# First units of an HGRN2 and maxout-FFN kernel: two tokens a partition in the loads, x from outputs by tokens, and half FFN steps placed among units 2 and 3

## The chip, the cores and the metric

The kernel runs on one core of a Trainium2 chip. The metric is the device time of one execution in microseconds (us). The kernel before took 477.63 us (median of 3 runs, 477.24 to 480.0). All times below are from those runs or from one profiled execution.

## What is computed

A gated linear recurrence for 4 batches and 8 heads over 768 tokens with heads of 48 features; its outputs, gathered to `x` of 3072 tokens by 384, go through a feed-forward network (FFN) that takes the maximum of three products.

```python
f = 1.0 / (1.0 + np.exp(-f_logit))
for t in range(S):
    state = f[:, :, t, :, None] * state + np.einsum('bhd,bhe->bhde', k[:, :, t], v[:, :, t])
    y[:, :, t] = np.einsum('bhd,bhde->bhe', q[:, :, t], state)
x = np.ascontiguousarray(y.transpose(0, 2, 1, 3)).reshape(B * S, H * D)
h = np.maximum(np.maximum(x @ w1, x @ w2), x @ w3)
return h @ w_out
```

The weights are 384 by 768 (three of them) and 768 by 384, and arrive as 64-bit floats.

## The kernel before

**Units and groups.** The tokens are cut into 24 units. Unit u is chunk u // 2 of 64 tokens of the two batches 2(u % 2) and 2(u % 2) + 1, all heads. Four units make a group of 512 tokens. Each group has its own `xT` (features on partitions, tokens along the free axis) and its own FFN, which runs while the units of the next group are computed.

**One unit.** `load` brings f, k and q, `load_v` brings v. For units 0 to 7 (`u < BY_ROWS`) a load has tokens on partitions, `transposed` (L274) turns each of f, k and q by four TensorE transposes of 128x128 (L278) into PSUM, and later units are turned by VectorE instead. `sigmoids` (L295) makes the gate; `scan` and `before` run the two scans of VectorE (L316, L334); `after` makes kh (L327), `keys` transposes it on TensorE (L354) and copies it to ks. `pairs` multiplies kh and qh (L379) and masks the result to `at` (L382). `values` multiplies v with `at` (L393) and ks with v (L402) into one PSUM tile y, and adds the new state (L408, L410). `finish` adds the part of the old state (L423) and ScalarE copies y, feature by token, into `heads` in three pieces (L429).

**Packing.** In `heads` the features of a head lie on partitions 0 to 47 or 64 to 111. `pack` (L437) moves them to the dense feature order of `xT` by ten DMA transfers (L445). For group 0 units 0 and 1 are packed by one call and units 2 and 3 by another, all on the SP queue. In every later group `pack(0, 2)` comes after the third unit's `finish` and `pack(3, 3, xT, both)` after the fourth's, alternately on the queues of SP and ScalarE, five each.

**The FFN as a generator.** `ffn(g, xT)` (L453) issues its work in steps: for each of six column blocks j and three weights i three matmuls (L472) of 128x512, with a ScalarE copy (L477) or a VectorE maximum (L479) after them; then four output blocks of six matmuls (L497), each with a copy (L500) and two output DMAs (L505). A full step counts as two yields, an output block as two, so a group from the second on has 18 x 2 + 4 x 2 = 44. Group 0 does the blocks j = 0 and 1 in 12 half steps of 256 tokens, one yield each, first those of units 0 and 1, then those of units 2 and 3, so it has 12 + 12 x 2 + 8 = 44 yields as well. In group 0 each step also rounds weights (`round_begin` on ScalarE, L232; `round_end` on VectorE, L239 and L240, and GpSimd, L246) and issues the loads of more of them (`load_weights`, L208, 12 buffers).

**The order.** `tc.manual_schedule()` keeps the order of the code on each engine; nothing is reordered. `pending` holds the FFN generators in order and `fill(n)` takes n yields from the first; when it ends, the next begins. Units 0 to 3 are written out by hand (L535 to L602). There `busy(n)` puts in matmuls whose result is not used. Before the loop come `fill(6)`, `fill(2)`, `fill(2)`. The loop over u from 4 takes in each of the units 4 to 7 seven yields (2, 2, 2 and 1); in unit 8 eight, of which none is ahead of its `keys`; then 12 in odd and 10 in even units. The head of one turn of the loop sets where the next group's FFN may begin:

```python
fill(0 if u == 2 * GRP else 4 if u % 2 and u > 2 * GRP else 2)
...
    finish(u - 1)
    ...
    elif u % GRP == 0:
        pack(3, 3, xT, both)
if u % GRP == 0:
    if u > GRP:
        pending.append(ffn(u // GRP - 1, xT))
...
pairs(u)
...
fill(2)
```

After the loop come `fill(2)`, `finish(23)`, the last `pack(3, 3, xT, both)`, the last FFN appended, and `fill(12)`.

**Queues.** Nearly all DMAs are issued by SP in the order of the code; an SP instruction that waits holds all that follow. DMAs of SP and ScalarE take eight landing semaphores in turn, and an issue waits until the transfer that last had its semaphore has landed. Nine of the first weight loads go by GpSimd's queue (L571, L589, L594).

Of the kernel before, what the change touches and what calls it, by code (L numbers as in the profile page):

```python
# [9 lines left out]
FP32 = mybir.dt.float32  # L10
# [36 lines left out]
C = 64  # L47
DP = 64
# [7 lines left out]
def kernel(  # L56
# [32 lines left out]
    def fast():  # L89
        ctx = ExitStack()  # L90
        with ctx:
# [47 lines left out]
            ROOM = H * DP  # L139
            NAMES = "fkq"  # L140
            room = {nm: [keep.tile([128, 2 * ROOM], FP32, name=f"{nm}_ld{i}") for i in range(2)] for nm in NAMES}
            slots = {nm: [room[nm][u // 2][:, u % 2 * ROOM:(u % 2 + 1) * ROOM] for u in range(4)] for nm in NAMES}
            rows = {nm: [t.rearrange("t (h d) -> t h d", d=DP) for t in slots[nm]] for nm in NAMES}
            blocks = {nm: [t.rearrange("p (n h d) -> p n h d", n=C // 32, d=32) for t in room[nm]] for nm in NAMES}
            for nm in NAMES:
                for t in room[nm]:
                    nc.vector.memset(t.rearrange("p (h d) -> p h d", d=DP)[:, :, D:], 0.0)
# [10 lines left out]
            act = (nc.scalar, nc.scalar)  # L158

            def load_tokens(dst, src, u, queues=one):  # L160
                c, bp = divmod(u, 2)
                for a in range(2):
                    queues[a].dma_start(out=dst[a * C:(a + 1) * C, :, 0:D],  # L163
                                        in_=src[2 * bp + a, :, c * C:(c + 1) * C, :].rearrange("h t d -> t h d"))

            def load(u, queues=one, names="fkq"):
                for nm, src in (("f", f_logit), ("k", k), ("q", q)):
                    if nm not in names:
                        continue
                    if u < BY_ROWS:  # L170

                        c, bp = divmod(u, 2)
                        queues[NAMES.index(nm) % 2].dma_start(  # L173
                            out=rows[nm][u % 4][:, :, 0:D],
                            in_=src[2 * bp:2 * bp + 2, :, c * C:(c + 1) * C, :].rearrange("b h t d -> t b h d"))
                    elif u % 2 == 0:
                        t0 = u // 2 * C
                        for n in range(C // 32):
                            for par in range(2):
                                for e0, w in ((0, 32), (32, D - 32)):  # L180
                                    p0 = par * DP + e0
                                    nc.sync.dma_start(  # L182
                                        out=blocks[nm][u // 2 % 2][p0:p0 + 32, n, :, 0:w],
                                        in_=src[:, par::2, t0 + n * 32:t0 + (n + 1) * 32, e0:e0 + w].rearrange(
                                            "b h t d -> t (b h) d"))

            def load_v(u, queues=one):
                load_tokens(v_tiles[u % NLD], v, u, queues)
# [85 lines left out]
            def transposed(nm, u, name="tr"):  # L274

                t = {"tr": ps_tr, "p": ps_f}[name].tile([128, HP, 2, C], FP32, name=name)
                for hp in range(HP):
                    nc.tensor.transpose(t[:, hp].rearrange("p a t -> p t a"), slots[nm][u % 4][:, hp * 128:(hp + 1) * 128],  # L278
                                        ident)
                return t.rearrange("p h a t -> p a h t")  # L280
# [105 lines left out]
            def values(u):  # L386
# [3 lines left out]
                for hp in range(HP):  # L390
                    for par, a in FOUR:
                        o, s = (par ^ a) * DP, slice(a * C, (a + 1) * C)
                        nc.tensor.matmul(y[o:o + DP, a, hp * C:(hp + 1) * C], lhsT=v_ld[s, 2 * hp + par, :],  # L393
                                         rhs=d["at"][s, par, hp, :], start=(hp == 0),
                                         stop=False, skip_group_check=True)
                if u < NU - 2:

                    Y = HP * C
                    for hp in range(HP):
                        for par, a in FOUR:  # L400
                            s = slice(a * C, (a + 1) * C)
                            nc.tensor.matmul(y[par * DP:(par + 1) * DP, a, Y + hp * D:Y + (hp + 1) * D],  # L402
                                             lhsT=d["ks"][s, 2 * hp + par, :], rhs=v_ld[s, 2 * hp + par, 0:D],
                                             start=False, stop=(hp == HP - 1), skip_group_check=True)
# [6 lines left out]
                d["y"] = y  # L411

            heads = keep.tile([128, HP, TOK], FP32, name="heads")

# [22 lines left out]
            def pack(u0, u1, xT, queues=one, half=None):  # L437

                t, n = slice(u0 * UT, (u1 + 1) * UT), 0
                to = xT[:, :, t] if half is None else by_halves(xT)[:, half]  # L440
                for h in range(H):
                    for lo, hi in ((h * D, min(h * D // 128 * 128 + 128, h * D + D)), (h * D // 128 * 128 + 128, h * D + D)):
                        if lo < hi:
                            p0 = h % 2 * DP + lo - h * D
                            queues[n % len(queues)].dma_start(out=to[lo % 128:lo % 128 + hi - lo, lo // 128, :],  # L445
                                                    in_=heads[p0:p0 + hi - lo, h // 2, t])
                            n += 1
# [86 lines left out]
            with tc.manual_schedule():  # L534
                load(0, both)  # L535
                load(1, (nc.scalar, nc.sync))
                load_v(0)
                load(2, one, "f")
                load_v(1)
                load(2, one, "kq")  # L540
                load(3)
                load_v(2)
                load_v(3)
                xT = new_xT()
# [13 lines left out]
                keys(1)  # L558
                scan(2)
                after(2)  # L560
                pairs(1)
                finish(0)
                carry(2)
                before(2)
                sigmoids(3)
                busy(2)
                values(1)
                keys(2)
                scan(3)
                after(3)  # L570
                load_weights(6, queue=nc.gpsimd)  # L571
                pairs(2)
                finish(1)
                carry(3)
                pack(0, 1, xT, one, 0)
                load(GRP, one, "fk")
                before(3)
                busy(2)
                values(2)
                keys(3)  # L580
                round_begin(0)
                finish(2)
                pairs(3)
                round_end(0)
                busy(2)
                round_begin(1)
                round_begin(2)
                round_end(1)
                load_weights(2, queue=nc.gpsimd)  # L589
                values(3)  # L590

                nc.tensor.transpose(ps_tr.tile([128, 128], FP32, name="tr"), ident, ident)
                round_end(2)
                load_weights(1, queue=nc.gpsimd)  # L594
                finish(3)
                round_begin(3)
                pack(2, 3, xT, one, 1)
                load_weights(3)
                load(GRP, one, "q")
# [3 lines left out]
                pending.append(ffn(0, xT))  # L603
# [8 lines left out]
                for u in range(GRP, NU):  # L612
# [18 lines left out]
                    if BY_ROWS <= u + 3 < NU and u % 2:  # L631
                        load(u + 3, one, "fkq" if u % GRP == 1 else "f")
# [13 lines left out]
                    if BY_ROWS <= u + 2 < NU and u % GRP == 0:  # L646
                        load(u + 2, one, "k")
# [9 lines left out]
                    if BY_ROWS <= u + 2 < NU and u % GRP == 0:  # L657
                        load(u + 2, one, "q")
# [270 lines left out]
```

## Time and profile before

| what | value |
|---|---|
| median of 3 runs | 477.63 us (477.24 to 480.0) |
| profiled execution: its time, its span | 478.4 us, 476.7 us |
| TensorE busy (PE) | 456.6 us, 96% of the span |
| VectorE, ScalarE, GpSimd busy | 270.4 us, 146.0 us, 109.9 us |
| FFN matmuls L472, L497 | 293.1 us, 96.3 us |
| transfers xT<-heads, all | 120 |
| HBM read, written | 37.75 MB, 4.72 MB |

PE is TensorE's matmul side, PEld its weight loads, DVE VectorE, ACT ScalarE, POOL GpSimd, SP the engine that issues most DMAs; a "q" behind the name means the engine's instruction queue (waits and DMA issues). Views that the prediction uses: the slices (the span in 40 parts, digits are tenths busy), the windows (busy us of each engine in a stretch, with the granted TensorE clock), the timeline (start us, us, engine, line, operation, tiles, count, and in brackets the idle time before it and what ended it) and the chain of waits (start us, us, what). A 32-bit matmul stands in the trace as two records, a TensorE transpose as one: `L379 x32` is 16 matmuls, `L278 x4` four transposes, `L472 x6` one step.

### The profile page before, as it was taken

The page shows a single profiled execution, that of the slowest core. Times are in us where ns is not written, and L with a number is a line of the kernel's source. Part 1 is how long each engine was busy: PE and PEld are TensorE (multiplying, and loading weights), DVE is VectorE, ACT ScalarE, POOL GpSimd, SP SyncE. Part 2 cuts the span into 40 slices and gives each one's busy share as a digit, 9 for nine tenths or more (in the row PEclk, how much of TensorE's full clock was granted, in tenths as well). Part 3 has the DMA queues.
Part 4 walks back from the last instruction along what each step waited for, and adds up shares of the span by engine and source line. Part 5 has one row for each costly group of instructions (what it writes and reads, how often), then busy time and mean ns, then how long its engine had stood idle before and what let it go on. Part 6 is the DMA issues. An engine that isn't in the chain of part 4 may idle for free.

```text
span 476.7 us, 10276 instructions
## 1 busy us (share of the span) xinstructions
PE 456.6 (96%) x4063; PEld 247.9 (52%) x4063; DVE 270.4 (57%) x528; ACT 146.0 (31%) x343; POOL 109.9 (23%) x134
## 2 busy tenths in 40 slices
PE   4969799999999999999999999999999999999995
PEld 3748655556445445544446544455554445444453
DVE  5976776767487584587685577694584220021110
ACT  2443467522012133244243243243243211100000
POOL 2283544441230230320330321330321300000000
PEclk9988999999999999999999999999999999999999
DMA  9996998614466544476635477534470011100002
GB/s 133 137 286 190 219 331 124 95 45 70 91 96 93 144 81 114 87 141 87 159 72 121 82 144 88 161 71 116 84 147 3 1 51 44 40 1 0 2 17 52
DMA packets 175637, 47.92 MB, mean 101 GB/s; under 512 B 155136, under 2 KB 173184, under 8 KB 175584
## 3 DMA queue, kind: packets, MB, share of 16 engines
q1 hardware_dynamic: 170016, 42.50, 46.5%
q0 software_dynamic: 1008, 3.54, 2.5%
q10 hardware_dynamic: 4560, 1.18, 1.4%
q8 instruction: 33, 0.54, 0.5%
q14 instruction: 20, 0.16, 0.1%
HBM read 37.75 MB, written 4.72 MB: 89 GB/s over the span
## 4 chain that ended last, share of the span: by engine, by line
PE 87%; SPq 6%; DMA 4%; issue 1%; ACT 1%; DVE 0%; POOL 0%; ACTq 0%; DVEq 0%
PE p L472 56%; PE p L497 20%; PE y L393 3%; PE y L423 2%; PE a L379 2%; SPq L182 2%; PE y L402 2%; DMA f_ld<-in_f_logit_dram 2%; SPq L173 1%; DMA xT<-heads 1%; SPq L445 1%; DMA q_ld<-in_q_dram 1%; PE tr L278 1%; SPq L163 1%; PE tr L354 0%
## 5 line engine op out<-in xcount | busy, mean ns | idle before, releaser
L472 PE MATMUL p<-xT,w_in 128*128 128x512 f32 (+1 forms) x684 | 293.1, 580 | 4.1 <-DMA xT<-heads 2.2
L472 PEld LDWEIGHTS p<-xT,w_in 128*128 128x128 f32 x684 | 127.9, 192 | 139.9 <-issue 127.2
L497 PE MATMUL p<-w_out,hm 128*128 128x384 f32 x288 | 96.3, 489 | 0.0
L479 DVE TENSOR_TENSOR top<-p,top 128x512 f32<-128x512 f32 (+1 forms) x38 | 24.9, 656 | 107.5 <-PE p L472 107.5
L497 PEld LDWEIGHTS p<-w_out,hm 128*128 128x128 f32 x288 | 54.0, 190 | 37.6 <-issue 1.9
L369 DVE STREAM_TRANSPOSE ks<-kh 32x128 f32<-32x128 f32 x224 | 67.7, 302 | 3.6
L477 ACT COPY top<-p 128x512 f32<-128x512 f32 (+1 forms) x38 | 21.3, 562 | 149.5 <-PE p L472 149.5
L326 POOL COPY ends<-r 128x8 f32<-128x8 f32 x24 | 6.5, 272 | 189.0 <-DVE r L316 189.0
L479 DVE TENSOR_TENSOR hm<-p,top 128x512 f32<-128x512 f32 (+1 forms) x38 | 24.7, 651 | 30.0 <-PE p L472 30.0
L429 ACT COPY heads<-y 64x256 f32<-64x256 f32 (+1 forms) x72 | 26.5, 369 | 45.6 <-PE y L423 39.1
L327 POOL TENSOR_TENSOR kh<-kt,r 128x512 f32<-128x512 f32 x16 | 31.3, 1959 | 36.5 <-DVE kt L283 23.9
L500 ACT COPY o<-p 128x384 f32<-128x384 f32 x24 | 11.4, 476 | 86.8 <-PE p L497 83.0
L316 DVE TENSOR_TENSOR_SCAN r<-gate,from_one 128x520 f32<-128x520 f32 x24 | 30.3, 1262 | 10.1 <-ACT gate L295 6.1
L334 DVE TENSOR_TENSOR_SCAN prod<-gate,from_inv 128x520 f32<-128x520 f32 x24 | 31.0, 1291 | 0.0
L246 POOL TENSOR_TENSOR w_in<-top_bits,rest_bits 128x384 uint32<-128x384 uint32 x18 | 18.5, 1030 | 26.9 <-DVE top_bits L242 12.1
L382 DVE TENSOR_TENSOR at<-a,mask 128x512 f32<-128x512 f32 x24 | 16.6, 690 | 11.6 <-PE a L379 11.2
L393 PEld LDWEIGHTS y<-at,v_ld 64*64 64x64 f32 x768 | 13.4, 134 | 15.5 <-issue 10.2
L344 POOL TENSOR_TENSOR state<-st,ends 128x384 f32<-128x384 f32 x22 | 19.8, 902 | 0.1
L283 DVE STREAM_TRANSPOSE gate<-sig 128x512 f32<-128x512 f32 x16 | 11.3, 705 | 14.4 <-ACT sig L298 14.4
L338 POOL TENSOR_TENSOR qh<-qt,prod 128x512 f32<-128x512 f32 x16 | 18.8, 1175 | 2.3 <-DVE qt L283 2.3
L423 PEld LDWEIGHTS y<-qh,state 48*48 48x48 f32 x704 | 11.3, 119 | 13.8 <-issue 11.6
L393 PE MATMUL y<-at,v_ld 64*64 64x64 f32 x768 | 16.7, 224 | 0.0
(79 smaller groups left out, 308.8 us busy)
## 6 DMA issues: line engine op xcount, KB each, us to landing
raw<-in_moe_w_dram SPq DMA_DIRECT2D x27, 384.0 KB, 4.9
v_ld<-in_v_dram SPq DMA_DIRECT2D x48, 96.0 KB, 3.4
raw<-in_moe_w_out_dram SPq DMA_DIRECT2D x12, 384.0 KB, 6.4
out_dram<-o SPq DMA_DIRECT2D x47, 96.0 KB, 2.2
raw<-in_moe_w_dram POOLq DMA_DIRECT2D x9, 384.0 KB, 7.1
xT<-heads SPq DMA_DIRECT2D x30, 72.0 KB, 2.2
f_ld<-in_f_logit_dram SPq DMA_DIRECT2D x32, 64.0 KB, 2.6
k_ld<-in_k_dram SPq DMA_DIRECT2D x32, 64.0 KB, 2.5
```

What stands on the lines that cost most here:

```text
L316: nc.vector.tensor_tensor_scan(r[:, 0:LEN][:, ::-1], flat(gate)[:, ::-1], flat(from_one)[:, ::-1], 1.0, op0=ALU.mult, op1=ALU.max)
L327: (nc.vector if u < BY_ROWS else nc.gpsimd).tensor_tensor(kh.rearrange("p h a t -> p a h t"), kt, by_batch(r[:, 1:LEN + 1].rearrange("p (x ...
L334: nc.vector.tensor_tensor_scan(flat(prod), flat(gate_tiles[u % 2]), flat(from_inv[u % 2]), 1.0, op0=ALU.mult, op1=ALU.max)
L344: nc.gpsimd.tensor_tensor(t, states[u % 2], ends[:, u, :].unsqueeze(2).to_broadcast([128, 2 * HP, D]), op=ALU.mult)
L369: nc.vector.transpose(ks[n * 32:(n + 1) * 32, :, par, e0:e0 + 32], kh[p0:p0 + 32, :, a, t0:t0 + 32])
L393: nc.tensor.matmul(y[o:o + DP, a, hp * C:(hp + 1) * C], lhsT=v_ld[s, 2 * hp + par, :], rhs=d["at"][s, par, hp, :], start=(hp == 0), stop=F ...
L423: nc.tensor.matmul(y[o:o + D, a, hp * C:(hp + 1) * C], lhsT=st[r, a, hp, :], rhs=d["qh"][r, a, hp, :], start=False, stop=(hp == HP - 1), s ...
L429: nc.scalar.copy(heads[o, :, t0 + a * C:t0 + (a + 1) * C], y[i, a, 0:HP * C].rearrange("p (h t) -> p h t", h=HP))
L472: nc.tensor.matmul(p if g or w < TOK else p.rearrange("p (two t) -> p two t", two=2), lhsT=w_in[i][:, kt, j * 128:(j + 1) * 128], rhs=rhs, ...
L477: nc.scalar.copy(top, p)
L479: nc.vector.tensor_tensor(hm[:, j, t] if i == 2 else top, p, top, op=ALU.max)
L497: nc.tensor.matmul(p[:, 0:DM], lhsT=hm[:, j, i * UT:(i + 1) * UT], rhs=w_out[:, j, :], start=(j == 0), stop=(j == NJ - 1))
```

## The change

Line numbers move: L278 becomes L282, L379 L383, L393 L398 or L402, L402 L423, L423 L447 or L465, L429 L471, L445 L486, L472 L513, L497 L538.

1. **Loads of f, k and q for units 0 to 7.** A partition holds two neighbouring tokens of all heads: runs of 96 numbers instead of 48, on 64 partitions instead of 128. The two units of a chunk share one tile, unit parity choosing the half of the partitions.
2. **`transposed`.** It becomes 16 ordinary matmuls of 64x64 with the identity as moving operand, per head pair, token of the two and head parity, instead of four transposes of 128x128.
3. **Group 0's way to x.** `values` makes y by tokens for units 0 to 3; the new state's part moves to `sums`, into a tile of its own; `finish_by_tokens` adds the old state's part after a matmul of 1x1, copies y to SBUF (L450), transposes it by three TensorE transposes (L454) and copies it into `xT` (L455). The 20 packing transfers of group 0 go.
4. **The written-out order.** The loads, the weights (all nine early ones on SP now) and the rounding move; six of FFN 0's half steps go in by `fill(1)` among units 2 and 3, and `fill(6)` after them stays. Of the four `busy` calls two are left, with one matmul each.
5. **The loop** keeps its `fill` counts; only the names of the queue arguments change.

```diff
-            ROOM = H * DP
+            ROOM = 2 * H * DP
...
+            twos = {nm: [t[:, 0:2 * H * D].rearrange("p (h e) -> p h e", h=H) for t in room[nm]] for nm in NAMES}
...
-                        queues[NAMES.index(nm) % 2].dma_start(
-                            out=rows[nm][u % 4][:, :, 0:D],
-                            in_=src[2 * bp:2 * bp + 2, :, c * C:(c + 1) * C, :].rearrange("b h t d -> t b h d"))
+                        queue.dma_start(
+                            out=twos[nm][c % 2][bp * C:(bp + 1) * C],
+                            in_=src[2 * bp:2 * bp + 2, :, c * C:(c + 1) * C, :].rearrange(
+                                "b h (g two) d -> g b h (two d)", two=2))
...
+                r = slice(bp * C, (bp + 1) * C)
                 for hp in range(HP):
-                    nc.tensor.transpose(t[:, hp].rearrange("p a t -> p t a"), slots[nm][u % 4][:, hp * 128:(hp + 1) * 128],
-                                        ident)
+                    for n in range(2):
+                        for par in range(2):
+                            x0 = (hp * 4 + par * 2 + n) * D
+                            to = t[par * DP:(par + 1) * DP, hp].rearrange("p a (g two) -> p two g a", two=2)
+                            nc.tensor.matmul(to[:, n], lhsT=room[nm][c % 2][r, x0:x0 + DP], rhs=ident[r, r],
+                                             start=True, stop=True)
...
+                        if u < GRP:
+                            nc.tensor.matmul(y[s, par, hp * D:(hp + 1) * D], lhsT=d["at"][s, par, hp, :],
+                                             rhs=v_ld[s, 2 * hp + par, 0:D], start=(hp == 0),
+                                             stop=False, skip_group_check=True)
+                            continue
...
+            def finish_by_tokens(u, xT):
+                d = ready.pop(u)
+                y = d["y"]
+                if u >= 2:
+                    new = states[u % 2][:, 0, 0:1]
+                    nc.tensor.matmul(ps_f.tile([1, 1], FP32, name="p"), lhsT=new, rhs=new, start=True, stop=True)
+                    st = d["state"].rearrange("p (a h) d -> p a h d", a=2)
+                    for hp in range(HP):
+                        for par, a in FOUR:
+                            r = slice(par * DP, par * DP + D)
+                            nc.tensor.matmul(y[a * C:(a + 1) * C, par, hp * D:(hp + 1) * D], lhsT=d["qh"][r, a, hp, :],
+                                             rhs=st[r, a, hp, :], start=False, stop=(hp == HP - 1), skip_group_check=True)
+                x = work.tile([UT, DM], FP32, name="o", bufs=3)
+                nc.scalar.copy(x.rearrange("t (hp par d) -> t par hp d", hp=HP, par=2),
+                               y[:, :, 0:HP * D].rearrange("t par (hp d) -> t par hp d", d=D))
+                tr_x = ps_tr.tile([128, NK, UT], FP32, name="tr")
+                for kt in range(NK):
+                    nc.tensor.transpose(tr_x[:, kt, :], x[:, kt * 128:(kt + 1) * 128], ident)
+                nc.scalar.copy(by_halves(xT)[:, u // 2, :, u % 2 * UT:(u % 2 + 1) * UT], tr_x)
...
-                finish(1)
+                round_begin(3)
                 carry(3)
-                pack(0, 1, xT, one, 0)
-                load(GRP, one, "fk")
+                load(GRP, nc.sync, "fk")
+                pending.append(ffn(0, xT))
+                fill(1)
                 before(3)
-                busy(2)
+                fill(1)
                 values(2)
                 keys(3)
-                round_begin(0)
-                finish(2)
+                sums(2)
+                fill(1)
+                finish_by_tokens(2, xT)
+                fill(1)
                 pairs(3)
...
+                fill(1)
                 values(3)
...
-                finish(3)
-                round_begin(3)
-                pack(2, 3, xT, one, 1)
-                load_weights(3)
-                load(GRP, one, "q")
+                fill(1)
+                sums(3)
+                finish_by_tokens(3, xT)
+                load(GRP, nc.sync, "q")
                 load_v(GRP)
                 load(GRP + 1)
                 load_v(GRP + 1)
-                pending.append(ffn(0, xT))
                 fill(6)
```

## The prediction, made before the changed kernel ran

> **What bounds the kernel now.** I read the page first, then the windows of the first 60 us, then the timeline at the places where one group's FFN ends and the next begins, and last the chain of waits for durations.
>
> The page, busy times and slices:
>
> ```profile
> PE 456.6 (96%) x4063; PEld 247.9 (52%) x4063; DVE 270.4 (57%) x528; ACT 146.0 (31%) x343; POOL 109.9 (23%) x134
> ...
> PE   4969799999999999999999999999999999999995
> ```
>
> TensorE is the bound. Each slice is 11.9 us; what is not 9 lies in the first five (60 us). After that a change pays only in TensorE work, and any TensorE wait that is new there costs its whole length.
>
> Windows of the early stretch (length, busy us of each engine with instruction counts, granted clock, DMA share, GB/s):
>
> ```profile
> 24.00:30.00 6.00, 4.97 (x198) 4.03 (x199) 4.57 (x8) 2.72 (x6) 4.64 (x6) 1.00 0.93 292
> 30.00:36.00 6.00, 3.30 (x53) 1.91 (x46) 3.89 (x6) 2.21 (x5) 5.20 (x6) 0.77 1.08 285
> ...
> 29.90:33.30 3.40, 1.88 (x58) 1.15 (x50) 3.08 (x6) 2.10 (x5) 3.03 (x4) 1.00 1.04 303
> 33.30:36.70 3.40, 2.22 (x5) 1.37 (x6) 0.91 (x1) 0.11 (x1) 2.17 (x3) 0.50 1.14 261
> 36.70:40.10 3.40, 3.40 (x10) 2.65 (x9) 0.57 (x2) 1.69 (x4) 0.00 (x0) 0.50 0.96 262
> ```
>
> TensorE was busy 1.88 of 3.40 us, and the granted clock fell to 0.50 for 6.8 us, until a stretch of 3.4 us was full. From the step that began at 35.67 to 40.10 it ran 4.4 us at half rate: 2.2 us lost.
>
> The timeline where FFN 0 ends and FFN 1 begins (unit 8):
>
> ```profile
> 108.61 0.66 PE L423 MATMUL y<-qh,state 48*48 48x64 f32 x32 [0.78 <-DVE st L410]
> 109.34 1.14 ACT L429 COPY heads<-y 128x256 f32<-128x256 f32 x3 [2.07 <-PE y L423]
> 109.67 8.01 PE L497 MATMUL p<-w_out,hm 128*128 128x384 f32 x24
> 110.51 3.21 ACTq L445 DMA_DIRECT2D xT<-heads  x5
> 118.95 4.10 SPq L445 DMA_DIRECT2D xT<-heads  x5
> 122.66 3.87 PE L472 MATMUL p<-xT,w_in 128*128 128x512 f32 x8
> ```
>
> And at the last such place:
>
> ```profile
> 397.72 11.88 PE L497 MATMUL p<-w_out,hm 128*128 128x384 f32 x36
> 397.86 1.14 ACT L429 COPY heads<-y 128x256 f32<-128x256 f32 x3
> 399.01 3.98 SPq L445 DMA_DIRECT2D xT<-heads  x5
> 399.03 3.69 ACTq L445 DMA_DIRECT2D xT<-heads  x5
> 409.44 2.74 PE L472 MATMUL p<-xT,w_in 128*128 128x512 f32 x6
> ```
>
> The last unit of a group ends on TensorE at 109.3 and 397.8. Then follow three copies (1.2 us) and ten packing transfers, whose last issue ends 13.8 and 5.2 us after that end and which land about 2 us after issue (L445: 1.7 to 2.8 us at unit 8). TensorE does not notice, as three output blocks (3 x 4 us) are left over from the FFN before: they are the cover.
>
> **The change, part by part.** The sum is made on the profiled execution (478.4 us, span 476.7), 0.8 above the median; the prediction is for the median.
>
> *(a) The order's yields: the cover goes.* Before: 10 yields ahead of the loop and 7 in each of units 4 to 7, 38 of FFN 0's 44; the six left are the three blocks above. After: six `fill(1)` more, 16 + 28 = 44, nothing left. From unit 8 to unit 12's `finish` the loop takes 8 + 12 + 10 + 12 + 2 = 44, again a whole FFN, and so on: nothing is left at units 8, 12, 16, 20 and at the end. The instruction order of the changed kernel as built says the same: behind `finish` come `pairs` (0.47 us) and then L513 on the new `xT`. So TensorE waits five times for copies, issue and landing, and behind it the next `values` and all of that FFN.
>
> How long: counted from the end of `finish`, copies to 1.2; ScalarE's five issues begin then, 0.6 us each, first landing at 1.2 + 2.1 = 3.3. SP's five issues are held by the eight landing semaphores: as built, at unit 8 four output DMAs stand ahead of the packs and wait for ScalarE's first four packs, so the packs begin at 5.95; at 12 the first pack waits for ScalarE's first, 3.4; at 16 and 20 one output DMA waits for it, packs at 3.95; at the end nothing holds them, 1.2. The first matmul of a step needs SP's first two packs, that is start + 1.2 (0.6 at the end, where the output DMAs are long gone: I take 0.9) + 2.1; `pairs` hides 0.45. Waits: 8.2, 5.6, 6.3, 6.3 and 4.3: **+31 us**. Low bound: 4.3 everywhere, 21. High: packs as late as before (13.8 + 2 - 0.5 at unit 8, and 10 to 12 at three more), some 55.
>
> *(b) The clock after each wait.* By the windows, 1.5 us without work in 3.4 were enough. Each of the five waits would do it, and half rate then lasts to the end of the first full stretch, 3.4 to 6.8 us after the restart (4.4 above); half of about 4.8 is lost, 2.4 each: **+12 us**, bounds 0 and 17. The Trainium skill, "TensorE: Matmul & The Clock Gate", Part 1, names an idle window of 3.4 us, free-running, as the condition; by that only about 3.6 of the five waits would hold a whole idle window, 8.6 us in place of 12. The row, where 1.88 us of work did not help, decides for me.
>
> *(c) The 16 matmuls in place of four transposes.* The chain of waits has the prices:
>
> ```profile
> 59.08 0.59 PE tr L278 x4
> ...
> 62.24 0.88 PE tr L278 x8
> ...
> 65.69 0.62 PE y L393 x32
> ```
>
> A unit pays 0.59 (f) + 0.88 (k and q) = 1.47. Sixteen 64x64 matmuls are 32 records, 0.62 in L393, but there four quarters of the array work at once; single records of the trace show rounds of four every 58 ns. The new ones all read one half of the rows, so only two column halves can overlap: 16 rounds x 58 ns = 0.93, + 0.15 to start = 1.08, and 2.0 for k and q: 3.1 a unit. Units 5 to 7 stand on TensorE's path: 3 x 1.65 = **+5 us**. Low bound the pace of four (1.7 a unit, +1), high no overlap (2.0 each, 6.0 a unit, +14); I take the middle since two records of one row half do start 7 ns apart in L393. The skill speaks against the change here: "TensorEngine Tiling (Array Packing)", Tile-to-Partition Mapping, Restrictions, says that column tiling excludes transpose mode for 32-bit data, so these are full multiplications; the trace shows one record for a transpose and two for a matmul, as the count of 32 has it.
>
> *(d) The early stretch.* Transfers: in 6 to 24 us loads of 192-byte runs moved at about 163 GB/s, weights of 1024-byte runs later at about 335. 384-byte runs lie between 163 and 326 (a packet at the same price); through both rows I get some 235, so a load of 196 KB takes 0.85 instead of 1.2 us. f of unit 0 comes some 0.5 us sooner (5.9 before), and the order then is f2 at 12, f3 at 13, three weights by 16.5, k2 at 17.3 and q3 at 20. That is no bound: VectorE is. A unit costs it 1.23 + 0.21 + 0.65 + 1.23 + 0.69 + 0.68 = 4.7 us, and before it worked so from 7.8 to 27.7. After, nine roundings (0.35 + 0.56), four maxima (0.42) and two state sums (0.56) stand among them: 18.8 + 8.2 + 1.7 + 1.1 = 29.8 from 7.3 at best, 37.1. With waits for k2 (1 us) and for TensorE (3.5) I put the last state sum of unit 3 at 41.6. TensorE has done the six half steps by then (6 x 1.3 us beside VectorE). Then 1x1 matmul, old state (0.66), copy (0.5), three transposes (0.45), copy (0.5) to 43.7; each waits for the one before, and the half steps stand behind them on TensorE. Six half steps (7.8) and f and k of unit 4 (2.2) to 53.7, q (1.1) 54.8. Before, 12 half steps and the same three transposes were done at 58.0. **-3 us**, bounds -8 (VectorE never waiting) and +3.
>
> What the packing and its 20 SP issues (0.6 each) cost before is in this: the wait at 32.3 to 35.7, and q of unit 4, which held TensorE from 49.0 to 50.7. q now stands behind eleven weight loads on SP, three before; they cost 1.3 us each and SP waits for rounded buffers (the last at about 37), so it lands near 48, hidden until 55. If rounding is late, q is the next to wait. The weights' move from GpSimd's queue to SP puts k2 to v3 behind three of them (3.8 us), counted above. Two ScalarE copies a unit instead of three, and `busy` gone: nothing, ScalarE is 31% busy and TensorE waits for VectorE there.
>
> *Sum:* 31 + 12 + 5 - 3 = +45. 478.4 + 45 = 523.4 for the profiled execution, **523** for the median.
>
> **The rivals.**
> 1. *Packs as late as before* (SP stays held by other transfers). For: SP's last issue ends 13.8 us after `finish` at unit 8, 10.7 at 12. Against: as built, less stands ahead of the packs. High end of (a): +22, about 545.
> 2. *Full price of the matmuls*, no overlap of column halves: +9, about 532.
> 3. *The early gain is nil*, TensorE's half steps waiting for weights: +3 to +8, about 529.
> 4. *Clock not throttled*: -12, about 511.
> 5. *Not slower: the cover isn't needed.* If the packs landed within 2 us of `pairs` at all five places, without a throttle, 10 us would be paid against an early gain of 8 and transposes at +1: about 480. It decides from a wait of some 1.4 us per place down. Against it: the copies alone end 1.2 us after `finish` and no transfer of L445 landed sooner than 1.7.
>
> **How the numbers follow.** My forecast (waits of 4 to 9 us, throttled) has 0.60; rival 1 0.12, 2 0.06, 3 0.07, 4 0.10, 5 and anything like it 0.05. Range: 505 (rival 4 with the better early stretch) to 545 (rival 1); 0.8 lies within. About 1% (5 us) is what a measurement of this kernel tells from no change: slower by more 0.95, within 0.03, faster 0.02.
>
> **What would show it.** In the changed profile: (a) idle of L513 put down to xT<-heads at five places, 4 to 9 us each, and no L538 between `finish` and L513; (b) a granted clock of 0.5 after each; (c) L282 32 records in about 1.1 us; (d) the first full step of FFN 0 at about 54, before 59.5. It would be wrong if L513 follows `pairs` within 2 us, or if (d) comes before 45.

## The result, and the profile after

The changed kernel took 541.56 us (median of 4 runs, 540.46 to 543.67) against 478.2 us of the kernel before on the same chip: a ratio of 1.1325, 95% interval 1.1272 to 1.1378. The profiled execution took 543.67 us (span 541.9); all positions below are in it, and the span has grown by 65.2 us. Forecast were 523 us and +45. Single runs of one kernel below differ by up to 10 us (e11: 528.03 to 538.39); that the clock opened at another time in them is likely, but only one run of each kernel has a trace.

The page after, busy times, slices and clock:

```profile
PE 495.5 (91%) x4740; PEld 277.9 (51%) x4740; DVE 267.8 (49%) x528; ACT 145.7 (27%) x339; POOL 103.0 (19%) x125
...
PE   6999899999749999959999879999779999799996
...
PEclk9999799999969999989999979999979999889999
```

A slice is now 13.5 us. Where all digits behind the first five but the last were 9, there are now five notches, each with a lower clock at or just behind it. The first slices are fuller than before, which looks good and is not: TensorE is busy there because it is slow.

What TensorE waited for after (engine, line and tile, what ended the wait: us in total, times, longest):

```profile
PE p L513 <- DMA xT<-heads: 25.3, 4, 10.2
PE p L513 <- ACT rest_bits L264: 5.9, 1, 5.9
PE tr L282 <- DMA f_ld<-in_f_logit_dram: 4.7, 1, 4.7
PE tr L454 <- ACT o L450: 3.2, 4, 1.0
```

The first two lines are the five waits at the group boundaries: 10.2, 5.6, 5.9, 5.7 and 3.7 us, 31.1 in all. The 5.9 "ACT rest_bits" is one of them as well: a wait for several semaphores, put down to the last one.

The timeline at the first boundary after, which answers to the lines of unit 8 before:

```profile
144.91 0.66 PE L465 MATMUL y<-qh,state 48*48 48x64 f32 x32 [0.78 <-DVE st L431]
145.39 0.65 PE L383 MATMUL a<-qh,kh 48*64 48x64 f32 x32
145.64 1.14 ACT L471 COPY heads<-y 128x256 f32<-128x256 f32 x3 [2.02 <-PE y L465]
146.81 3.41 ACTq L486 DMA_DIRECT2D xT<-heads  x5
149.34 1.42 SPq L184 DMA_DIRECT2D v_ld<-in_v_dram  x2
150.85 2.50 SPq L546 DMA_DIRECT2D out_dram<-o  x4
153.45 3.12 SPq L486 DMA_DIRECT2D xT<-heads  x5
156.22 7.36 PE L513 MATMUL p<-xT,w_in 128*128 128x512 f32 x12 [10.18 <-DMA xT<-heads]
```

`finish` ends at 145.57 (before: 109.27), no output block (L538) stands behind `pairs`, and TensorE waits until 156.22. SP issues its packs only from 153.45, behind the loads and four output DMAs.

The windows around that wait (length, busy us of PE, PEld, DVE, ACT and POOL, granted clock, DMA share, GB/s):

```profile
146.00:150.00 4.00, 0.04 (x4) 0.00 (x0) 3.11 (x9) 0.74 (x3) 0.00 (x0) 1.00 0.60 81
150.00:160.20 10.20, 3.98 (x5) 1.85 (x6) 5.81 (x10) 0.63 (x1) 4.07 (x4) 0.50 0.45 96
160.20:165.00 4.80, 4.80 (x73) 2.46 (x72) 0.86 (x2) 0.59 (x1) 0.00 (x0) 1.00 0.76 94
```

The clock falls during the wait and stays at half for 4.0 us of work after it. The other boundaries have 2.85, 5.40, 3.43 and 5.84 us of work at half clock: 21.5 us, of which half is lost, 10.7.

The early stretch after, TensorE's timeline:

```profile
4.71 1.97 PE L282 MATMUL tr<-ident,f_ld 64*64 64x64 f32 x32 [4.71 <-DMA f_ld<-in_f_logit_dram]
...
19.37 1.98 PE L398 MATMUL y<-v_ld,at 64*64 64x48 f32 x32
...
41.27 2.93 PE L513 MATMUL p<-xT,w_in 128*128 128x256 f32 x6
44.13 1.15 PE L282 MATMUL p<-ident,q_ld 64*64 64x64 f32 x32
45.21 1.56 PE L513 MATMUL p<-xT,w_in 128*128 128x256 f32 x6
46.70 1.17 PE L398 MATMUL y<-v_ld,at 64*64 64x48 f32 x32
...
63.16 10.43 PE L513 MATMUL p<-xT,w_in 128*128 128x256 f32 x36 [0.57 <-ACT xT L455]
73.53 1.15 PE L282 MATMUL tr<-ident,f_ld 64*64 64x64 f32 x32
74.51 1.10 PE L282 MATMUL tr<-ident,k_ld 64*64 64x64 f32 x32
```

The same six records of L513 take 2.93 us at 41.3 and 1.56 at 45.2; 32 records of L282 1.97 and 1.15, of L398 1.98 and 1.17. Up to 44.15 the clock is cold. The view of windows shows 1.00 there, but only because the trace's first clock record is that of 44.15: durations of one shape are the better witness. Before, L278 fell from 1.09 to 0.60 us by 13.7, and the first record stands at 12.8. And TensorE does not rest in this time:

```profile
4.70:23.40 18.70, 18.69 (x330) 16.93 (x330) 9.97 (x13) 2.96 (x5) 0.57 (x3) 1.00 1.22 211
23.40:44.10 20.70, 18.69 (x278) 15.53 (x274) 11.49 (x17) 5.64 (x12) 7.33 (x7) 1.00 0.97 248
```

It is busy 37.4 of 39.4 us (first busy column), VectorE 21.5 (third). The 2.0 us of idle time are two waits for the copy of L450, 1.01 us each; none is for a load. The twelve half steps end at 73.6 and f and k of unit 4 at 75.6, where 53.7 was forecast.

Behind the last waits of unit 3 the clock falls once more (columns as above; the granted clock is the third number from the end):

```profile
57.50:61.20 3.70, 2.36 (x71) 1.69 (x69) 2.68 (x5) 0.04 (x1) 1.88 (x2) 1.00 0.60 162
61.20:68.00 6.80, 5.74 (x14) 4.37 (x15) 0.13 (x1) 2.76 (x7) 1.00 (x1) 0.50 1.13 194
```

That is 5.74 us of work at half rate, 2.9 us lost, and no idle time ahead of it is longer than 1.23 us.

**The balance in spans.** Up to the end of unit 7's `finish` the changed kernel stands 36.3 us behind (145.57 against 109.27), with three output blocks more done (3 x 3.97 us): 24.4 us lost, 2 forecast. From there to the end it takes 396.3 us; before 367.4 less those 11.9, 355.5: 40.8 lost, 43 forecast.

### The profile page after: what moved, and what is told of

Same layout as the page of the kernel before. It is cut to its first block, busy times and chain, and to the rows that moved or that the text cites. A ratio compares the mean times of both kernels' runs of the same rounds, so it can differ in the third digit from the quotient of the medians.

```text
span 541.9 us, 11586 instructions
## 1 busy us (share of the span) xinstructions
PE 495.5 (91%) x4740; PEld 277.9 (51%) x4740; DVE 267.8 (49%) x528; ACT 145.7 (27%) x339; POOL 103.0 (19%) x125
## 4 chain that ended last, share of the span: by engine, by line
PE 91%; DMA 3%; ACT 2%; issue 1%; SPq 1%; ACTq 1%; DVE 0%; DVEq 0%
PE p L513 56%; PE p L538 17%; PE tr L282 3%; DMA xT<-heads 2%; PE p L282 2%; PE y L402 2%; PE y L465 2%; PE a L383 2%; PE y L423 2%; PE y L398 1%; PE tr L358 1%; ACTq L486 1%; ACT heads L471 1%; DMA f_ld<-in_f_logit_dram 1%; PE tr L454 1%
## 5 line engine op out<-in xcount | busy, mean ns | idle before, releaser
L513 PE MATMUL p<-xT,w_in 128*128 128x512 f32 (+1 forms) x684 | 305.0, 600 | 31.7 <-DMA xT<-heads 25.3
L513 PEld LDWEIGHTS p<-xT,w_in 128*128 128x128 f32 x684 | 132.5, 199 | 171.7 <-issue 145.2
L538 PE MATMUL p<-w_out,hm 128*128 128x384 f32 x288 | 95.3, 488 | 0.0
L538 PEld LDWEIGHTS p<-w_out,hm 128*128 128x128 f32 x288 | 54.2, 190 | 38.0 <-issue 2.4
L331 POOL TENSOR_TENSOR kh<-kt,r 128x512 f32<-128x512 f32 x16 | 31.4, 1962 | 36.2 <-DVE kt L287 28.5
L471 ACT COPY heads<-y 64x256 f32<-64x256 f32 (+1 forms) x60 | 22.1, 369 | 44.9 <-PE y L465 43.7
L243 POOL TENSOR_TENSOR w_in<-top_bits,rest_bits 128x384 uint32<-128x384 uint32 x18 | 21.3, 1188 | 50.7 <-DVE top_bits L239 23.6
L338 DVE TENSOR_TENSOR_SCAN prod<-gate,from_inv 128x520 f32<-128x520 f32 x24 | 29.5, 1230 | 0.0
L348 POOL TENSOR_TENSOR state<-st,ends 128x384 f32<-128x384 f32 x22 | 18.7, 849 | 0.2
L402 PEld LDWEIGHTS y<-at,v_ld 64*64 64x64 f32 x640 | 11.2, 134 | 14.1 <-issue 8.8
L383 PE MATMUL a<-qh,kh 48*64 48x64 f32 x768 | 17.9, 231 | 0.0
L282 PE MATMUL tr<-ident,f_ld 64*64 64x64 f32 x256 | 12.7, 266 | 4.7 <-DMA f_ld<-in_f_logit_dram 4.7
```

Of the source, the lines that this page charges most:

```text
L282: nc.tensor.matmul(to[:, n], lhsT=room[nm][c % 2][r, x0:x0 + DP], rhs=ident[r, r], start=True, stop=True)
L331: (nc.vector if u < BY_ROWS else nc.gpsimd).tensor_tensor(kh.rearrange("p h a t -> p a h t"), kt, by_batch(r[:, 1:LEN + 1].rearrange("p (x ...
L338: nc.vector.tensor_tensor_scan(flat(prod), flat(gate_tiles[u % 2]), flat(from_inv[u % 2]), 1.0, op0=ALU.mult, op1=ALU.max)
L383: nc.tensor.matmul(p[t, par, hp * C:(hp + 1) * C], lhsT=kh[r, hp, a, :], rhs=qh[r, a, hp, :], start=True, stop=True)
L471: nc.scalar.copy(heads[o, :, t0 + a * C:t0 + (a + 1) * C], y[i, a, 0:HP * C].rearrange("p (h t) -> p h t", h=HP))
L513: nc.tensor.matmul(p if g or w < TOK else p.rearrange("p (two t) -> p two t", two=2), lhsT=w_in[i][:, kt, j * 128:(j + 1) * 128], rhs=rhs, ...
```

## The experiments

The theory has two halves. At the boundaries the missing cover makes the waits, and the waits make the half clock. In the first units the new 64x64 work is dear and keeps the clock cold, so that TensorE, not VectorE, sets the pace. The rivals: the waits come from the new order of transfers; the early loss comes from loads, order or VectorE.

A mark that all kernels but those of e4 and e12 show is used below: the start of the 0.78 us wait ahead of unit 7's `finish`. It stands at 107.83 us before and at 144.13 after (132.2 without the three blocks).

**e1, the cover put back into the changed kernel.**

```
                 load_v(GRP + 1)
-                fill(6)
                 sigmoids(GRP)
```

> The changed kernel without the six W_ih0 matmul steps' call to fill that it has ahead of its loop, so that three output blocks are left over as cover at each group boundary, as the kernel before had them. Theory (the missing cover makes the five waits, and with them the clock's half-speed stretches there): the five idle times of 10.2, 5.6, 5.9, 5.7 and 3.7 us (31.1 in all) and some 10 us of half clock go, so 541.6 - 41 = about 500 us. Rival (the waits come from the new order of the transfers, not from the cover): the waits stay and the time is within 3 us of 541.6.

Measured: 503.37 us (494.92 to 504.24; profiled 504.08). TensorE's waits of over 0.6 us in the whole span:

```profile
PE tr L282 <- DMA f_ld<-in_f_logit_dram: 5.8, 1, 5.8
PE tr L454 <- ACT o L450: 3.2, 4, 1.0
PE p L442 <- DVE st L431: 1.2, 1, 1.2
PE y L465 <- DVE st L431: 0.8, 1, 0.8
```

No line of L513 is left, and from 73.0 us to 499.7 the clock is never low. One line of the order is worth 38 us by the medians (one of its runs took 494.92, the other three 502.65 to 504.24). By the profiled spans behind unit 7's `finish` it is worth 42: e1 takes 366.0 us there, 354.1 without the three blocks of 11.9, against 396.3.

**e4, only the cover taken from the kernel before.**

```
-                    fill(0 if u == 2 * GRP else 4 if u % 2 and u > 2 * GRP else 2)
+                    fill(6 if u == 2 * GRP else 4 if u % 2 and u > 2 * GRP else 2)
```

> The kernel before with only its cover at the group boundaries used up early: six more steps of fill at the first output unit, nothing else. Theory (cover): waits of about 31 us in all and 10 us of half clock appear at the five boundaries: 478 + 41 = about 519 us, with nothing changed ahead of the boundaries. Rival (the boundaries do not need it): 478.

Measured: 512.12 us, ratio 1.0704 (1.0658 to 1.075). TensorE's waits:

```profile
PE p L472 <- DMA xT<-heads: 13.2, 4, 5.7
PE p L472 <- ACT rest_bits L267: 11.5, 2, 5.8
```

The cause is confirmed from the other side; the size is 7 us under the forecast. The five waits are 3.5, 5.8, 5.7, 5.7 and 3.7: the last four as in the changed kernel, the first 6.7 us shorter. At that place the wait is set by when SP comes to the packs, 121.58 here, 1.2 us after `finish`, and 153.45 after, 7.9 behind it.

**e12, one output block of cover in place of three.** The same edit as e4 with `fill(4` for `fill(6`.

> The kernel before with four steps of fill at the first output unit, where e4 had six and the kernel before none: one output block (4 us) is left as cover at each boundary. Theory (cover shortens each wait by its own length, and an idle time below 2 us does not bring the half clock, as in e11): the waits of e4 of 3.5, 5.8, 5.7, 5.7 and 3.7 us become 0, 1.8, 1.7, 1.7 and 0, no half clock: 478.5 + 5 = 483 to 485. Rival (the half clock comes with any wait here): 10 us more, 490 to 495; rival 2 (the transfers begin later by as much as the cover is, the waits stay): 505 to 512.

Measured: 511.01 us, ratio 1.0683 (1.0645 to 1.072). My theory fell, and the time is that of rival 2. The waits did not simply stay: they are 6.8, 4.5, 5.8, 5.7 and 0.6 us, the first longer than in e4 and the last shorter. One output block of cover bought 1 us, which is within the noise of the two. SP's queue at the second boundary of e12 (`finish` ends at 198.10):

```profile
192.58 1.22 SPq L505 DMA_DIRECT2D out_dram<-o  x2
193.85 8.07 SPq L257 DMA_DIRECT2D raw<-in_moe_w_dram  x2
202.02 2.40 SPq L505 DMA_DIRECT2D out_dram<-o  x4
204.52 3.25 SPq L445 DMA_DIRECT2D xT<-heads  x5
```

Two weight loads take 8.1 us, 7.1 of it in a wait for packing transfers (SP's waits say "SPq L257 <- DMA xT<-heads: 7.1, 1, 7.1"). Behind them stand the output DMAs, and behind these the packs, from 204.52. In e4 the same five packs are issued from 201.25, 3.6 us after `finish`; here 6.4. At the first boundary the packs begin 8.7 us after `finish` (125.03), in e4 1.2. The cover moved other transfers to where they hold the packs up.

**e3, the loads and transposes of the kernel before in the changed kernel.**

```
-            room = {nm: [keep.tile([128, ROOM], FP32, name=f"{nm}_ld{i}") for i in range(2)] for nm in NAMES}
+            room = {nm: [keep.tile([128, 2 * ROOM], FP32, name=f"{nm}_ld{i}") for i in range(2)] for nm in NAMES}
...
-                            nc.tensor.matmul(to[:, n], lhsT=room[nm][c % 2][r, x0:x0 + DP], rhs=ident[r, r],
-                                             start=True, stop=True)
+                    nc.tensor.transpose(t[:, hp].rearrange("p a t -> p t a"), slots[nm][u % 4][:, hp * 128:(hp + 1) * 128],
+                                        ident)
```

> The changed kernel with the row loads and the four 128x128 transposes of the kernel before (undoes the two-tokens-a-partition loads with their 64x64 transposes; the rest of the change stays). Theory A (64x64 work keeps the clock cold and is dear in itself): the clock opens near 13 us, the first stretch is some 12 us shorter, units 4 to 7 some 6 us: 522 to 525. Theory B (only the price of the transposes counts): the clock still opens late and the time is 530 to 533. Rival (the first loads bind): no gain or a loss, 541 to 548.

Measured: 522.11 us, ratio 1.0897 (1.0851 to 1.0942): theory A. The clock opens at 11.6 us, and the mark stands at 121.92, that is 22.2 us earlier. TensorE waits 8.8 us for loads of f, k and q here and 4.7 in the changed kernel, so it is not the new loads that cost. TensorE's timeline in e3:

```profile
10.74 1.03 PE L275 MATMUL p<-ident,k_ld 128*128 128x128 f32 x4
11.71 0.69 PE L376 MATMUL a<-qh,kh 48*64 48x64 f32 x32
12.34 0.66 PE L275 MATMUL p<-ident,q_ld 128*128 128x128 f32 x4
```

**e6, the new loads and transposes alone in the kernel before** (e3's edit the other way round).

> The kernel before with only the new loads (two tokens a partition) and the 16 matmuls of 64x64 in place of four transposes, its order untouched. Theory (64x64 work is dear and keeps the clock cold): the clock opens after 25 us or later, the twelve half steps end 8 to 14 us after 58.0, units 4 to 7 pay 5 to 6 us more: 478 + 14 to 20 = 492 to 498. Rival (the clock is cold in the changed kernel because of its order, not of its 64x64 work): the clock opens near 13 us, 484 to 487.

Measured: 491.27 us, ratio 1.0276 (1.0225 to 1.0327), 1 us below the theory's lower end. The clock opens at 22.6 and the mark stands at 120.28, 12.5 us late. So the 64x64 work costs, and keeps the clock cold for 10 us longer, in the old order too. Up to 20 us e6 runs nearly what the changed kernel runs by then. The first difference is `values`, 1.13 us in the old form where the changed kernel's L398 takes 1.98:

```profile
20.03 1.13 PE L400 MATMUL y<-at,v_ld 64*64 64x64 f32 x32
```

The clock opens 1.5 us after it; the count under e7 says what that can have to do with it. Loads and transposes cost 12.5 us alone and 22.2 in the new order.

**e5, what is left of the change:** outputs by tokens and half steps, with the edits of e1 and e3.

> The changed kernel with both of the large costs taken out: no six yields ahead of the loop (cover kept, as in e1) and the loads and transposes of the kernel before (as in e3). What is left of the change is the outputs by tokens, the half steps among units 2 and 3 and their order. If the parts add up, 541.6 - 38.2 - 19.5 = 484 us. Theory (the first stretch gains nothing from the new way to x: in e3 the twelve half steps ended at 59.2 us, in the kernel before at 58.0): 480 to 484, no waits at the boundaries. Rival (the new way to x is a gain by itself): 470 to 475.

Measured: 480.49 us, ratio 1.0038 (1.0012 to 1.0064). What is left of the change loses 2 us, where the prediction had the early stretch, new loads included, win 3. Its mark is 3.8 us late.

**e2, full-array work ahead of the first unit.**

```
                 xT = new_xT()
+                busy(6)
                 sigmoids(0)
```

> The changed kernel with six full-array matmuls of 128x256 more, whose result is not used, ahead of the first sigmoids. Theory (a cold TensorE clock up to 33.65 us lengthens the first units): the clock opens by about 12 us, the half steps of units 2 and 3 end some 7 to 10 us earlier than 75.2 us, and the time is about 534. Rival (loads or VectorE set the first units): no gain, 541 to 545.

Measured: 538.35 us (531.09 to 539.12), ratio 1.1241 (1.1203 to 1.1279): a gain of 3 us in the median where 7 were expected, and its interval just overlaps with that of the changed kernel (1.1272 to 1.1378). The 33.65 us of the expectation should have been 44.15. In the profiled execution (531.09) the clock opens at 6.8, and its mark stands at 131.70, 12.4 us earlier:

```profile
2.28 5.05 PE L564 MATMUL p<-from_one,ident 128*128 128x256 f32 x12 [2.28 <-DVE from_one L114]
7.26 1.15 PE L282 MATMUL tr<-ident,f_ld 64*64 64x64 f32 x32
8.24 1.10 PE L282 MATMUL p<-ident,k_ld 64*64 64x64 f32 x32
```

The other four runs have no trace, but their mean granted clock is on record: 0.940 to 0.952 against 0.964 in the profiled one, that is 51 to 64 us at half clock against 38. So the clock was low again for longer in them; at which place isn't shown.

**e7, the same with 64 rows and 64 columns.**

```
+                p = ps_f.tile([128, TOK], FP32, name="p")
+                for _ in range(6):
+                    nc.tensor.matmul(p[0:64, 0:256], lhsT=ident[0:64, 0:64],
+                                     rhs=from_one.rearrange("p x t -> p (x t)")[0:64, 0:256], start=True, stop=True)
                 sigmoids(0)
```

> The changed kernel with six matmuls ahead of the first sigmoids as in e2, of the same 256 columns, but with 64 rows and 64 columns of the array in place of 128 and 128. Theory (what opens the clock is work that fills the array, not a busy TensorE): the clock does not open by 10 us; it opens as late as in the changed kernel, some 40 us or later, and the time is 540 to 545. Rival (any early work opens it): it opens near 7 us as in e2 and the time is 531 to 539.

Measured: 542.77 us (one run). TensorE is busy from 2.28 just as in e2, and the clock opens at 46.7:

```profile
2.28 4.92 PE L592 MATMUL p<-from_one,ident 64*64 64x256 f32 x11 [2.28 <-DVE from_one L114]
...
7.42 1.80 PE L282 MATMUL tr<-ident,f_ld 64*64 64x64 f32 x29
```

So in these two executions it was not the time for which TensorE is busy that opened the clock, but how much of the array the work used.

A count over all 14 traces says the same. In each of them the stretches between changes of the recorded clock are whole multiples of 3.41 us (17.07, 6.83, 81.92 and 10.24 us are the first in the changed kernel), so cut each trace into stretches of 3.41 us back from the first clock record. As array work take rows x columns x moving columns, summed over the matmul records of a stretch (one of `128*128 128x256` is 4.2 million). The stretch that ends where the clock opens holds 26.9 to 33.9 million in 13 of the 14 traces (33.9 in e2, 26.9 in e6, 27.6 in the changed kernel). The earlier ones hold at most 21.2, and in 35 of them TensorE is busy without a break. e11 is the exception: its clock opened behind 18.5. This was counted afterwards from traces made for other questions, and no run was made to test it.

The Trainium skill, "TensorE: Matmul & The Clock Gate", Part 1, says that about 3.4 us of sustained activity open it, with a free-running window. e2 agrees (4.5 us after the first matmul); the changed kernel, busy for 18.69 of 18.70 us from 4.70 on and still cold, doesn't, and the measurement decides.

**e9 and e11, TensorE kept busy through the waits.** `busy` behind `pairs` at the boundaries of the changed kernel, and ahead of the last FFN; e9 has 32, 16 and 10, e11 20, 11 and 7.

```
                     pairs(u)
+                    if u % GRP == 0 and u > GRP:
+                        busy(20 if u == 2 * GRP else 11)
...
                 pack(3, 3, xT, both)
+                busy(7)
```

> The changed kernel with matmuls whose result is not used put behind pairs at the five group boundaries (32 of 128x256 at the first, 16 at the next three, 10 at the last), shorter than the waits there. Theory (waits and clock are two costs: the transfers set the wait, the idle time sets the half clock after it): the next FFN steps begin as late as before, the half clock at the last four boundaries goes, some 10 us less in all: 531 to 534. Rival (the half clock is not due to the idle time, or the full price is the wait): 540 to 545.

Measured: 541.05 us, ratio 1.1298 (1.1233 to 1.1363). It decides nothing: one such matmul takes 0.44 us, not the 0.26 that I had reckoned with, so the filling (14.1 us at the first place) outlasts the waits.

> The run before it with shorter filling: one of these matmuls took 0.44 us, twice what was reckoned, so 32 and 16 of them were longer than the waits. Now 20 at the first boundary (8.8 us, wait 10.2), 11 at the next three (4.8 us, waits 5.6 to 5.9) and 7 at the last (3.1 us, wait 3.7). Theory (wait and clock are two costs, one behind the other): the next FFN steps begin within 0.3 us of the changed kernel's time after finish, no half clock at the boundaries, 541.6 - 10 = 531 to 533 us. Rival (the half clock costs nothing, as the FFN after it would have waited anyway): 540 to 543.

Measured: 534.78 us, ratio 1.12 (1.115 to 1.125), 2 us above the theory's range and 5 below the rival's. The first boundary of e11:

```profile
137.36 0.66 PE L465 MATMUL y<-qh,state 48*48 48x64 f32 x32 [0.78 <-DVE st L431]
137.84 0.65 PE L383 MATMUL a<-qh,kh 48*64 48x64 f32 x32
138.42 8.90 PE L564 MATMUL p<-from_one,ident 128*128 128x256 f32 x40
148.78 5.50 PE L513 MATMUL p<-xT,w_in 128*128 128x512 f32 x12 [1.46 <-DMA xT<-heads]
```

L513 begins 10.8 us after the end of `finish`, 10.65 in the changed kernel: the transfers set it. Its twelve records take 5.50 us where they took 7.36. No boundary has a half clock, though idle times of 0.5 to 1.9 us are left. From unit 7's `finish` to the end it takes 388.3 us instead of 396.3: the half clock cost 8 us by this count, 10.7 by the windows. The rest of the gap between its profiled time and the changed kernel's is the early clock, which opened at 22.1 here, in the same code.

**e8 and e10, towards a faster kernel.** e10 is the kernel before with e2's `busy(6)`; e8 is e5 with that, two unused matmuls in `finish_by_tokens` for units 0 and 1, and this:

```
+                load(2, nc.sync, "kq")
                 load_weights(3)
-                load(2, nc.sync, "kq")
                 load(3, nc.sync, "kq")
```

> The kernel before with six full-array matmuls of 128x256 more ahead of the first sigmoids, result unused, as in e2. Theory (the cold clock costs where TensorE sets the first units; in the kernel before VectorE sets them): the clock opens near 7 instead of 12.8 us, the twelve half steps end at most 1 us earlier, 477 to 478.5 us. Rival (the cold clock costs in this kernel too): 470 to 474.

> e5 (outputs by tokens, cover kept, loads and transposes of the kernel before) with three mends: six full-array matmuls ahead of the first sigmoids, k and q of unit 2 ahead of the first three weights on the SP queue, and two unused matmuls in the 1.0 us for which TensorE waits for the copy of units 0 and 1. Theory (e5 lost its gain to waits for k and q of unit 2 of 1.4 and 1.8 us and to half clock from 20 to 27 us): 3 to 6 us less than e5's 480.5, so 474.5 to 477.5, just below the kernel before. Rival (the chain of VectorE and copies sets the first units of this order, not the clock): 479 to 481.

Measured: e10 479.62 us, ratio 1.0016 (0.999 to 1.0043); e8 479.33, ratio 1.0015 (0.9993 to 1.0038). For e10 the theory holds within the noise, 1 us above its range: the clock opens at 5.4, and the twelve half steps end at 57.9 instead of 58.0. For e8 it fell: the waits for k and q of unit 2 are gone and the clock opens at 6.8, but the time is 1.2 us below e5's, not 3 to 6. Its FFN begins at 27.3 us, 4.3 earlier than before, and its twelve half steps still end at 58.8. No version here beats the kernel before.

## Why the prediction was wrong in size and right in direction

**(a) The waits: right.** 31.1 us measured and 31 forecast; singly 10.2, 5.6, 5.9, 5.7 and 3.7 against 8.2, 5.6, 6.3, 6.3 and 4.3. The first is 2 us longer since SP's packs began 7.9 us after `finish`, not 5.95. The sign named for it, 4 to 9 us at each place, was a little too narrow at both ends. By the terms that (a) states the waits would come to 8.8, 6.25, 6.8, 6.8 and 3.75, 32.4 in all; the list that it adds up is 1.7 us lower. e1 and e4 show the cause from both sides.

**(b) The clock after the waits: right.** 8 us (e11) to 10.7 us (windows), 12 forecast. Waits of 3.7 us brought the half clock, idle times up to 1.9 us in e11 did not. But the reading behind it, that 1.5 us without work in 3.4 are enough, is too simple. Before, 29.9 to 33.3 us held 1.88 us of work, 18.2 million by the count under e7, and the clock fell; in e11, 302.0 to 305.4 held 1.96 us, but 36.2 million, and it stayed.

**(c) The 16 matmuls in units 5 to 7: right.** 32 records take 1.15 us at full clock, 1.08 forecast; the nine groups of those units take some 9.5 us against 5.1, +4.4 against +5.

**(d) The early stretch: wrong, and this is the whole miss.** Of the 24.4 us lost up to unit 7's `finish` 4.4 belong to (c), so (d) is +20 where -3 was forecast. The step that failed is "That is no bound: VectorE is", and after it the count that ended at 53.7; measured is 75.6, 22 us later, while the three other terms together are within 3 us. The first full step of FFN 0 begins at 75.5, where the sign named for it was about 54. Four things were left out.
- The clock was taken as open. I read the granted clock only where it falls, not where it first opens: at 12.8 us before, behind transposes of 128x128. The change replaced these by 64x64 work, and the clock opened at 44.15. In e2's profiled execution 12.4 us come back when it opens at 6.8; in e3 the mark comes 22.2 us earlier, by the clock and the price together, so by difference some 10 us are the price of the 64x64 work in units 0 to 7. This is an estimate from two executions; at full clock its 24 groups of 32 records cost 0.55 us more each (1.15 against 0.60), 13 us if nothing hides them.
- `values` by tokens is dearer: 1.17 us (1.98 cold) against 0.69. In the old form the four matmuls of a head pair use all four combinations of input half and output half (`o = (par ^ a) * DP`); in the new one input and output half are both `s`, so only two. I had used this very argument for the transposes in (c), and not here. It is argued from code and durations; no run isolates it.
- The chain of copy, transposes and copy in each `finish_by_tokens` makes TensorE wait (3.2 us at L454 in all). With (c) undone and the cover back, e5's mark is 3.8 us late where an earlier one was forecast.
- The half clock from 61.2 to 68.0 us, 2.9 us lost. (b) counted on it behind the five waits alone, and it came behind idle times of at most 1.23 us as well.

Rival 3 (the early gain is nil, 529) was nearest in kind, but its size was bounded by waits for weights, not by the clock. That 541.56 lies in the range is luck: rival 1, the packs as late as before, had put its top at 545, and that did not happen.

**What stays open.** The early clock does not always open at one place: it opened at 44 to 47 us in the profiled executions of the changed kernel, e1, e7 and e9, and at 22.1 in that of e11, with the same instructions ahead of it as in the changed kernel. The array work in a stretch of 3.41 us fits all of the traces but e11's, and no run here shows why that one opened.

## What to carry to other kernels

Where one engine is nearly full, leftover work of the last stage is not slack but the cover of the next stage's hand-over: count it before steps are moved ahead, and count it in what the DMA queue will do, for a third of the cover can be worth next to nothing (e12). Take the price of each small matmul at the clock that it will run at, and ask whether the new instructions still open the clock that the old ones opened. A fuller TensorE row in the slices isn't progress; compare durations of one shape.

## What the runs showed of the hardware that was not expected

- TensorE busy without a break for 18.7 us with mostly 64x64 matmuls did not raise its clock; 5.05 us of 128x128 matmuls did (e2, and likewise in e8 and e10), and 64x64 ones in their place did not (e7). In 13 of 14 traces the clock opened behind the first stretch of 3.41 us with at least 26.9 million of array work; earlier ones had at most 21.2.
- An idle wait of 3.7 us brought half clock for 5.8 us of work behind it; five idle times of 0.5 to 1.9 us, with filling work around them, brought none (e11). Without such work around them, idle times of at most 1.23 us were enough (the changed kernel at 61.2 us).
- A DMA issue that waits on its queue can hold back unrelated ones: two weight loads held SP for 8.1 us while they waited for packing transfers (e12).
